# RWKV-7 state and gated MLP on one core: loads of chunks 4 and 5 moved between DMA queues, and the order of the weight words

## The chip, the cores and the metric

The kernel runs on one core of a Trainium2 chip. The metric is device time in microseconds. The engines of a core are TensorE (PE in the profile, with its weight loads as PEld), VectorE (DVE), ScalarE (ACT), GpSimd (POOL) and SyncE (SP). They run their own instruction streams side by side and wait for each other by semaphores. A DMA is issued by the queue of one of the engines; SyncE does nothing else here.

## The reference

Inputs are r, k, v, w, a, b of shape (4, 8, 768, 40): four batches, eight heads, 768 time steps, head size 40. For each head a 40 by 40 state is carried through time:

```python
y[:, :, t] = np.einsum('bhd,bhde->bhe', rt, state)
Sa = np.einsum('bhde,bhe->bhd', state, at)
state_decay = state * wt[:, :, None, :] - np.einsum('bhd,bhe->bhde', Sa, bt)
state = state_decay + np.einsum('bhd,bhe->bhde', vt, kt)
```

The y of all heads, laid side by side, is x of 3072 tokens by 320. An MLP follows, with weights of 320 by 2048 and 2048 by 320:

```python
h = x @ w_in
g = h * np.cos(h)
return (g @ w_out).astype(np.float32)
```

The two weight matrices come as 64-bit floats, all other inputs as 32-bit floats.

## The kernel before

**Chunks.** Time is cut into 24 chunks of 32 steps. Inside a chunk the recurrence is turned into matrix products and a triangular inverse; between chunks only the state (tile `qz`) is carried. A chunk's work is in small steps. `p1` prepares pairs of chunks from w, a and b: transposes, the running product of w, 1/w (`over_w`, L393), b/w (`bn`), a times the running product (`aT`), and their products (`nps`). `by_blocks` or `inverse` then inverts on VectorE for four chunks at a time; for chunks 0 to 3 the inverse is made in 16 by 16 blocks (`pair_step`), and `pair_first` and `pair_second` put the off-diagonal block together on TensorE, by way of two helper tiles `half` and `rn`. `p2` takes v, r and k (`p2_in` L564, `p2_kn` L572 on GpSimd, then transposes and `gram`). `main` is the chain through the state: `ch_t` (sT), `ch_q` (qps), `ch_x` (x0ps), `ch_s` (sps), `ch_z` (dps, then qz and yt). `tokens` (L749) writes yt to DRAM (xd) and reads it back transposed (xT), as the MLP's input.

**The weights.** Each weight is made into a 32-bit float from the two 32-bit words of its 64-bit float. There are 20 pieces of 512 columns by 128 rows, 512 KB of words each: for the first quarter of the MLP pieces 0 and 1 (w_in), 2 (the tail of w_in) and 3 to 5 (w_out), and so on; pieces 18 and 19 are the last 1024 columns of w_out as the kernel lays them out. A piece goes through four steps (`rounded`, L224): `fetch` (the words, L237, on SyncE's queue), `taken` (L245, L246 on VectorE, L249, L251 on ScalarE), `mantissa` (L255 VectorE, L258 ScalarE) and `product` (L261 VectorE, then the sign on GpSimd, L264). The words lie in buffers lent by other tiles: pieces 0 and 1 in gT, 2 in nt, 3 in u, 4 in inv, 5 and 6 in gT again, 7 in nt, 8 in u, 9 in inv, and from 10 on nt, u and inv in turn. So a fetch waits until the lender, or the piece before it, has let the buffer go.

**Memory that is used twice.** The weights' places are empty at first, and hold other things. The w and a of chunks 2 and 3 lie in w_in's second half, their b in the last 1024 columns of w_out (`late_out`). `half0` and `rn0`, the helper tiles of the inverse of chunks 0 to 3, lie in the 1536 columns before these (`spare`, L119 to L121): half0 under pieces 13 and 14, rn0 under piece 15. The upper part of half0 is set to zero at the start (L122). For w, a and b of all other chunks there are two tiles each, for even and odd chunks, so chunk 4's loads overwrite what chunk 0 left.

**Loads.** `load(c, names, via)` (L150) issues four DMAs of 40 KB for each name, one per batch (L156). From chunk 4 on w is not read from the input but from a DRAM tile `wd`, in which running products over time have been made ahead (`ws_fetch` L163, `ws_scan` L170, `ws_store` L182, for four chunks at a time). A load of w of chunk 4 or 5 has therefore to wait for the landing of that store.

**Order.** The order of all instructions is written out by hand. `step(work, of_inv, of_w)` (L346) issues one piece of work, then what has come due, then so many steps of the inverse and of the weights. `later(n, work)` (L343) makes work come due after n more steps. `landed` (L577) puts the next chunk's k, v and r in the list once the old ones have been read. A prologue handles chunks 0 to 3's preparation and most of chunk 0; then the loop over chunks goes through a list of segments, in which `M` is a place for a piece of the MLP. Work on one engine is done in this order, and SyncE issues its DMAs in it: one that waits for a buffer holds all behind it.

**Around the change.** In the prologue, `both_a` of chunk 2 (L870) puts six loads of four DMAs each in the list: w of chunks 4 and 5 and a of 4 after 8 steps, a of 5 and b of both after 9 (L879). They come due before chunk 2's k, v and r, which are put there by `p2_in(1)` after L970, and before pieces 3 and 4 of the weight words, fetched after the inverse. `shifted` (L944) issues small matmuls whose result is unused (tile pad), 121 of them in the prologue and 75 in chunk 19 (L973); `busy` issues others, of 512 columns. Most matmuls stand in two helpers, so the profile gives them the lines L101 (`mm`) and L330 (`turned`).

Of the kernel before, what the change touches and what calls it, by code (L numbers as in the profile page):

```python
# [20 lines left out]
def kernel(  # L21
# [43 lines left out]
    nc = tc.nc  # L65
    B, H, S, D = r.shape
    P, C, DP = 128, 32, 64
    HH = H // 2
    NCH = S // C
    DM, DFF = moe_w_in.shape  # L70
    NF = DFF // P
# [41 lines left out]
    w_out_sb = const.tile([P, NF, DM], F32, tag="w_out", name="w_out_sb")  # L113
# [2 lines left out]

    late = DFF - 2 * H * DP
    late_out = w_out_sb.rearrange("p f n -> p (f n)")[:, NF * DM - 2 * H * DP :]
    spare = w_out_sb.rearrange("p f n -> p (f n)")[:, NF * DM - 2 * H * DP - 3 * P * 4 : NF * DM - 2 * H * DP]  # L119
    half0 = spare[:, : 8 * P].rearrange("p (n t) -> p n t", t=C)  # L120
    rn0 = spare[:, 8 * P :].rearrange("p (n t) -> p n t", t=C // 2)  # L121
    nc.gpsimd.memset(half0[:, :, C // 2 :], 0.0)  # L122
    nat = {}
    for n, fill in (("w", 1.0), ("a", 0.0), ("b", 0.0)):
        for i in range(4):
            x = slice((i - 2) * H * DP, (i - 1) * H * DP)
            if i < 2:
                t = const.tile([P, H, DP], F32, tag=f"nat_{n}{i}", name=f"nat_{n}{i}")
            else:
                t = {  # L130
                    "w": w_in_sb[:, 0, late:], "a": w_in_sb[:, 1, late:], "b": late_out
                }[n][:, x].rearrange("p (h d) -> p h d", h=H)
# [4 lines left out]
    for n in "kvr":  # L137
        t = const.tile([P, H, D], F32, tag=f"nat_{n}", name=f"nat_{n}")
# [11 lines left out]
    def load(c, names, via=nc.sync):  # L150
        for n in names:
            for i in range(B):
                at_c = src[n][i, :, c * C : (c + 1) * C, :]
                if n == "w" and c >= 4:
                    at_c = wd[c // 4][i, :, c % 4]
                via.dma_start(nat[n, c][blk[i], :, :D], at_c.rearrange("h t d -> t h d"))  # L156
# [186 lines left out]
    def later(steps, work):  # L343
        waiting.append([steps, work])

    def step(work, of_inv=0, of_w=0, small=False):  # L346


        before = list(waiting)
        work()  # L350
        G["small"] = small
        for w in before:
            w[0] -= 1
            if w[0] == 0:
                waiting.remove(w)
                w[1]()
        for steps, n in ((inv_steps, of_inv), (w_steps, of_w)):
            for _ in range(min(n, len(steps))):
                steps.pop(0)()
# [67 lines left out]
    def p1_b(c):  # L427
        ps = at("bT")
        for i in range(2):
            turned(ps[:, i], bn_b[(c + i) % 7])  # L430
        for i in range(2):
            bT = sb3.tile([P, 4, P], F32, tag="opT", name="bT")
            nc.scalar.copy(bT.rearrange("p j t -> p (j t)"), ps[:, i])
            G["bT", c + i] = bT
# [427 lines left out]
    def p1(c):  # L862


        def first_w():
            p1_w(c)
            if c == 4:
                later(1, lambda: load(6, "w"))

        def both_a():  # L870
            p1_a(c)
            if c == 4:
                later(1, lambda: load(7, "w"))
                for i in range(2):
                    later(1, lambda i=i: load(6 + i, "ab"))
            elif c >= 2 and c + 3 < NCH:
                for m in range(6):
                    later(
                        8 + m // 3 if c == 2 else (9 if c == 6 else 2) + m, lambda m=m: load(c + 2 + m % 2, "wab"[m // 2])  # L879
                    )  # L880

        return [first_w, both_a, lambda: p1_b(c), lambda: p1_n(c)]

# [23 lines left out]
    with tc.manual_schedule():  # L907
# [36 lines left out]
        def shifted(n):  # L944


            ps = at("pad")
            for _ in range(n):
                mm(ps[:1, 0, :1], idle[:, :1], idle[:, :1], True)
# [4 lines left out]
        first, other = p1(0), p1(2)  # L954
        for seg in (*first[:2], *other[:2], *first[2:], *other[2:]):
            step(seg)
        for m in range(2):
            w_work[m][0]()
        scanned(1)
# [10 lines left out]
        w_work[2][0]()  # L970
        p2_in(1)
        p2_kn(1)
        N_PAD = {0: 121, 19: 75}  # L973
        shifted(N_PAD[0])
        while inv_steps:
            inv_steps.pop(0)()
# [35 lines left out]
        for c in range(NCH):  # L1012
            t, q, x, s, z = main(c)
            v, k, g = p2(c + 1) if c + 1 < NCH else [lambda: None] * 3
            q0 = c - c % 4 + 4
            fill, pn, pn4, parts, blocks = (1, 4), None, None, [], []
            if c == 0:
                segs = []
            elif c == 1:
                parts = [parts0[0], parts0[1]]  # L1020
                segs = [t, parts[0], v, q, parts[1], k, x, g, s, z]
                fill = (1, 4)
            elif c == 2:
                parts = parts0[2:]
                segs, fill = [t, parts[0], v, q, k, M, x, M, parts[1], g, M, s, M, z, M, M], (0, 3)
            elif c == 3:
                pw4, pa4, pb4, pn4 = p1(4)
                pw, pa, pb, pn = p1(6)
                segs = [
                    t, pw4, M, q, pa4, M, x, lambda: scanned(2), M, s, pw, M, pb4, pa, M, pn4, M, z, M,  # L1030
                    pb, v, pn, k, M, g,
                ]
                fill = (2, 3)
            elif c == 4:
                pw, pa, *p8 = p1(8)
                blocks = [
                    lambda n=n, f=f: f(4, *n) for n in ((0, 1), (1, 4)) for f in (pair_first, pair_second)
                ]
                segs = [
                    t, v, M, q, M, k, x, M, blocks[0], M, blocks[1], M, s, blocks[2], M, pw, blocks[3], M, z, M,  # L1040
                    g, M, pa, lambda: scanned(3),
                ]
                fill = (2, 0)
            elif c == 5:
                pw, pa = p1(10)[:2]
                pb, pn = p8
                segs = [t, M, pb, q, M, pn, k, M, x, M, s, pw, v, M, z, M, g, M, pa, M]
            elif c % 4 == 0 and q0 < NCH:
                pb, pn = p1(q0)[2:]
                segs = [t, v, M, q, M, k, x, M, g, M, s, pb, M, z, M, pn, M, M]  # L1050
                if q0 + 4 < NCH:
                    segs.insert(-1, lambda: scanned(c // 4 + 2))
            elif c % 4 == 1 and q0 < NCH:
                pw, pa = p1(q0 + 2)[:2]
                segs = [t, M, pw, q, M, x, k, M, s, v, M, z, M, pa, M, g, M, M]
            elif c % 4 == 2 and q0 < NCH:
                pb, pn = p1(q0 + 2)[2:]
                segs = [t, M, pb, q, M, pn, v, M, x, M, s, k, M, g, M, z, M, M]
            elif c % 4 == 3 and q0 + 4 < NCH:
                pw, pa = p1(q0 + 4)[:2]  # L1060
                segs = [t, M, pw, q, M, x, k, M, s, v, M, z, M, pa, M, g, M, M]
            else:
                segs = [t, v, M, q, M, x, k, M, g, M, s, M, M, z, M, M]
            n = len(segs)

            goal = 8 * (c + 1) - (18 if c < 19 else 20)
            empty, places = 0, segs.count(M)
            if c > 3:
                empty = max(0, min(places - (goal - done), 2 if c < 8 else places))
                goal = max(goal, done + places - empty)  # L1070
            place = 0
            if c == 19:
                shifted(N_PAD[c])
            for i, seg in enumerate(segs):
                while seg is s and ("rt", c) not in G:
                    if allowed(c):
                        piece(4, 0)
                    else:
                        inv_steps.pop(0)()
                while seg is pn4 and w_steps:  # L1080
                    w_steps.pop(0)()
                if seg is not M:
                    step(seg, *((0, 0) if seg in parts else fill), small=seg in (q, x, g, s, z, pn, pn4, *blocks))
                    if seg not in parts and (c < 2 or c == 2 and not done):
                        busy({s: 6, q: 5, v: 4, k: 4, z: 4}.get(seg, 3))
                else:
                    place += 1
                    if place * empty // places > (place - 1) * empty // places:
                        continue
                    if allowed(c) and (c != 4 or done < 23):  # L1090
                        piece(*fill)
                while i == n - 1 and c > 3 and done < goal and c != 4 and allowed(c):
                    piece(*fill)
                if seg is pn and (c == 3 or c > 4 and c % 4 == 2):
                    inv_steps.extend(by_blocks(q0) if c == 3 else inverse(q0))
# [36 lines left out]
```

## Time and profile before

| What | us |
|---|---|
| Median of three runs (823.66 to 827.18) | 825.35 |
| The profiled execution | 821.18 |
| Its span, first to last instruction | 819.5 |
| TensorE busy in the span | 756.6 (92%) |
| VectorE busy | 484.4 (59%) |
| ScalarE busy | 386.5 (47%) |
| GpSimd busy | 198.5 (24%) |

All times inside the kernel are those of the one profiled execution, counted from its first instruction. In the profile's lines the first figures are start and duration, then the engine, the line of the kernel, the operation, the tile written and the tile read, and how many instructions the entry merges; what stands in brackets is the time that the engine had been idle before, and what ended it. "SPq" is SyncE's queue of DMAs; the duration there is the time of issuing, not of the transfer. "issue" is time in which an engine waited for nothing that the profile shows. The mean granted clock of TensorE is 0.955 of its full speed. Moved in all: 55.79 MB, 51.95 of them by SyncE's queue (q1), 0.98 by ScalarE's (q10), 0.33 by GpSimd's (q0).

### The profile page before, as it was taken

To read this page: it belongs to the slowest core of one execution; us is meant where nothing else is said; L and a number is where in the kernel's file an instruction comes from. 1 tells how busy PE (TensorE), PEld (TensorE's weight loads), DVE (VectorE), ACT (ScalarE), POOL (GpSimd) and SP (SyncE) were. 2 spreads that over 40 slices of the span, in tenths; PEclk is the share of its full clock that TensorE was granted. 3 is DMA by queue.
4 is the path that set the end of the run, shared out by engine and by line. 5 is a ranking of instruction groups with operands and counts; after the bars stand their busy time and mean duration, and the time that the engine had idled before them with its cause. 6 is when DMAs were issued, how large, how long until landed. Compare 5 with 4: busy or idle time off the path is not lost.

```text
span 819.5 us, 39690 instructions
## 1 busy us (share of the span) xinstructions
PE 756.6 (92%) x17858; PEld 580.2 (71%) x17858; DVE 484.4 (59%) x1025; ACT 386.5 (47%) x720; POOL 198.5 (24%) x354
## 2 busy tenths in 40 slices
PE   3676787999899999999999999999999999999997
PEld 2653456677677777787777877777787777777775
DVE  6956667866364698454796554895445873332231
ACT  1324566654254544446345445435635435363352
POOL 5214352430214123221230330330230222201000
PEclk9856687999999999999999999999999999999999
DMA  7536554254144323334224314214220212101000
GB/s 122 126 83 177 160 143 115 45 126 73 29 103 92 67 52 61 70 90 75 54 38 71 73 59 72 53 38 68 59 40 25 45 39 51 21 19 36 19 17 16
DMA packets 183304, 55.79 MB, mean 68 GB/s; under 512 B 157152, under 2 KB 178656, under 8 KB 183136
## 3 DMA queue, kind: packets, MB, share of 16 engines
q1 hardware_dynamic: 180560, 51.95, 29.2%
q8 instruction: 140, 2.29, 1.2%
q10 hardware_dynamic: 2320, 0.98, 0.6%
q0 software_dynamic: 256, 0.33, 0.2%
q14 instruction: 28, 0.23, 0.1%
HBM read 42.07 MB, written 11.14 MB: 65 GB/s over the span
## 4 chain that ended last, share of the span: by engine, by line
PE 63%; DVE 14%; DMA 6%; ACT 5%; SPq 5%; issue 5%; POOL 2%; DVEq 0%; ACTq 0%; POOLq 0%
PE ph L101 22%; PE po L101 18%; SPq L156 4%; PE x0ps L101 3%; PE dps L101 3%; PE gram L101 3%; DVE inv_tmp L480 2%; PE vT L330 2%; DVE rw L395 2%; DVE inv L484 2%; PE nps L101 2%; PE sps L101 2%; PE qps L101 2%; DMA words<-in_moe_w_out_dram 1%; PE sT L634 1%
## 5 line engine op out<-in xcount | busy, mean ns | idle before, releaser
L101 PE MATMUL po<-w_out_sb,gT 128*128 128x320 f32 x768 | 223.2, 439 | 0.0
L101 PE MATMUL ph<-xT,w_in_sb 128*128 128x256 f32 x768 | 188.7, 391 | 2.8 <-issue 2.5
L101 PEld LDWEIGHTS po<-w_out_sb,gT 128*128 128x128 f32 x768 | 140.2, 190 | 54.2 <-issue 1.7
L101 PEld LDWEIGHTS ph<-xT,w_in_sb 128*128 128x128 f32 x768 | 141.2, 193 | 32.9 <-issue 14.9
L806 ACT ACTIVATE turns<-ph,rnd 128x512 f32<-128x512 f32 x96 | 64.1, 686 | 159.0 <-PE ph L101 158.6
L808 DVE SCALAR_TENSOR_TENSOR turns<-turns,ph 128x512 f32<-128x512 f32 x96 | 64.0, 684 | 117.4 <-ACT turns L806 117.1
L816 DVE TENSOR_TENSOR gT<-ph,turns 128x512 f32<-128x512 f32 x96 | 65.7, 686 | 37.5 <-ACT turns L813 37.5
L733 POOL TENSOR_TENSOR qz<-qz,wc 128x160 f32<-128x160 f32 x92 | 41.7, 472 | 158.3 <-DVE qz L732 157.7
L813 ACT ACTIVATE turns<-turns,half_pi 128x512 f32<-128x512 f32 x96 | 69.3, 722 | 3.1
L812 ACT ACTIVATE turns<-turns 128x512 f32<-128x512 f32 x96 | 60.2, 627 | 16.8 <-DVE turns L808 16.8
L101 PE MATMUL ph<-xT,w_in_tail 64*128 64x256 f32 x384 | 55.8, 410 | 0.0
L484 DVE TENSOR_TENSOR inv<-inv,inv_tmp 128x31 f32<-128x31 f32 (+15 forms) x124 | 50.8, 410 | 4.3
L566 POOL COPY vp<-nat_v 128x320 f32<-128x320 f32 x25 | 12.2, 486 | 160.5 <-DMA nat_v<-in_v_dram 134.4
L732 DVE TENSOR_TENSOR qz<-dps,qz 128x160 f32<-128x160 f32 x92 | 28.9, 314 | 35.6 <-PE dps L101 35.3
L480 DVE TENSOR_TENSOR inv_tmp<-u,inv 128x31 f32<-128x31 f32 (+15 forms) x124 | 48.2, 389 | 2.3
L395 DVE RECIPROCAL rw<-nat_w 128x320 f32<-128x320 f32 x20 | 42.8, 2141 | 0.0
L638 ACT COPY s<-sT 128x512 f32<-128x512 f32 x46 | 24.5, 584 | 37.1 <-PE sT L634 37.0
L101 PEld LDWEIGHTS ph<-xT,w_in_tail 64*128 64x128 f32 x384 | 33.8, 190 | 9.4 <-issue 5.5
L744 POOL TENSOR_TENSOR yt<-yt,wb 128x512 f32<-128x512 f32 x24 | 31.4, 1309 | 22.4 <-DVE yt L739 22.4
L634 PE MATMUL sT<-ident,qz 128*128 128x128 f32 x184 | 26.6, 287 | 5.6 <-POOL qz L733 2.9
L396 POOL TENSOR_TENSOR bn<-nat_b,rw 128x320 f32<-128x320 f32 x22 | 19.5, 887 | 48.8 <-DVE rw L395 41.6
L698 DVE TENSOR_TENSOR sm<-sps,su 128x128 f32<-128x128 f32 x48 | 11.7, 285 | 31.9 <-ACT sm L693 31.9
(136 smaller groups left out, 1108.4 us busy)
## 6 DMA issues: line engine op xcount, KB each, us to landing
words<-in_moe_w_in_dram SPq DMA_DIRECT2D x8, 512.0 KB
nat_k<-in_k_dram SPq DMA_DIRECT2D x96, 40.0 KB
nat_v<-in_v_dram SPq DMA_DIRECT2D x96, 40.0 KB
nat_r<-in_r_dram SPq DMA_DIRECT2D x96, 40.0 KB
xd<-yt SPq DMA_DIRECT2D x48, 80.0 KB
out_dram<-ot SPq DMA_DIRECT2D x24, 160.0 KB
nat_b<-in_b_dram SPq DMA_DIRECT2D x88, 40.0 KB
wd<-ws SPq DMA_DIRECT2D x5, 640.0 KB
```

The costliest lines, as they stand in the source:

```text
L101: nc.tensor.matmul(o, lhsT=lhsT, rhs=rhs, start=start, stop=stop, skip_group_check=True)
L156: via.dma_start(nat[n, c][blk[i], :, :D], at_c.rearrange("h t d -> t h d"))
L395: nc.vector.reciprocal(rw, wn)
L480: nc.vector.tensor_tensor(tmp, u[:, j : j + 1, :j].to_broadcast([P, C - j, j]), x[:, j:, j : j + 1].to_broadcast([P, C - j, j]), ALU.mult,)
L484: nc.vector.tensor_tensor(x[:, j:, :j], x[:, j:, :j], tmp, ALU.subtract)
L634: nc.tensor.transpose(ps[:, i // 4, (i % 4) * P : (i % 4 + 1) * P], qz[:, i // 2, i % 2, C : C + P], ident)
L733: nc.gpsimd.tensor_tensor(z, z, wc.rearrange("p (f m b) -> p f m b", f=2, m=2)[:, :, :, bb] .unsqueeze(3).to_broadcast([P, 2, 2, D]), ALU. ...
L806: nc.scalar.activation(n, u, ACTF.Identity, bias=rnd, scale=1.0)
L808: nc.vector.scalar_tensor_tensor(n, n, -ROUND, u, ALU.add, ALU.subtract)
L812: nc.scalar.activation(n, n, ACTF.Abs)
L813: nc.scalar.activation(n, n, ACTF.Sin, bias=half_pi, scale=-2.0 * math.pi)
L816: nc.vector.tensor_tensor(gT[:, 2 * e : 2 * e + 2].rearrange("p f t -> p (f t)"), us[e], ns[e], ALU.mult)
```

## The change

The a and b of chunks 4 and 5, 16 DMAs, are issued by GpSimd instead of SyncE, behind its copies for chunk 1 (`p2_kn(1)`). The w of chunks 4 and 5, 8 DMAs, stay with SyncE and are put in the list in chunk 1: four after five steps and four after seven. So the words of piece 2, chunk 2's k, v and r, and the words of pieces 3 and 4 no longer stand behind these 24 loads. `half0` moves to the last 1024 columns of w_out, under pieces 18 and 19 and over the b of chunks 2 and 3, and is therefore set to zero after these have been read; rn0 stays under piece 15. The pad of the prologue has 115 matmuls in place of 121.

```diff
-    spare = w_out_sb.rearrange("p f n -> p (f n)")[:, NF * DM - 2 * H * DP - 3 * P * 4 : NF * DM - 2 * H * DP]
-    half0 = spare[:, : 8 * P].rearrange("p (n t) -> p n t", t=C)
-    rn0 = spare[:, 8 * P :].rearrange("p (n t) -> p n t", t=C // 2)
-    nc.gpsimd.memset(half0[:, :, C // 2 :], 0.0)
+    half0 = late_out.rearrange("p (n t) -> p n t", t=C)
+    rn0 = w_out_sb.rearrange("p f n -> p (f n)")[:, NF * DM - 2 * H * DP - P * 4 : NF * DM - 2 * H * DP]
+    rn0 = rn0.rearrange("p (n t) -> p n t", t=C // 2)
...
-            elif c >= 2 and c + 3 < NCH:
+            elif c > 4 and c + 3 < NCH:
                 for m in range(6):
-                    later(
-                        8 + m // 3 if c == 2 else (9 if c == 6 else 2) + m, lambda m=m: load(c + 2 + m % 2, "wab"[m // 2])
-                    )
+                    later((9 if c == 6 else 2) + m, lambda m=m: load(c + 2 + m % 2, "wab"[m // 2]))
...
         for seg in (*first[:2], *other[:2], *first[2:], *other[2:]):
             step(seg)
+        nc.gpsimd.memset(half0[:, :, C // 2 :], 0.0)
         for m in range(2):
             w_work[m][0]()
...
         p2_kn(1)
-        N_PAD = {0: 121, 19: 75}
+        for c in (4, 5):
+            load(c, "ab", nc.gpsimd)
+        N_PAD = {0: 115, 19: 75}
         shifted(N_PAD[0])
...
             elif c == 1:
                 parts = [parts0[0], parts0[1]]
                 segs = [t, parts[0], v, q, parts[1], k, x, g, s, z]
+                later(5, lambda: load(4, "w"))
+                later(7, lambda: load(5, "w"))
                 fill = (1, 4)
```

## The prediction

> **What bounds the kernel now.** I read the stages first (busy time by stretch), to see where time can be won at all:
>
> ```profile
> 40.00:52.00 12.00, 9.59 (x248) 6.61 (x237) 9.09 (x26) 2.32 (x5) 2.77 (x5) 0.64 0.43 102
> 64.00:84.00 20.00, 12.42 (x283) 7.53 (x285) 13.53 (x18) 11.43 (x20) 9.81 (x10) 0.67 0.64 180
> 107.00:127.00 20.00, 14.13 (x307) 9.55 (x299) 13.66 (x22) 14.84 (x27) 9.68 (x8) 0.91 0.59 154
> 200.00:400.00 200.00, 194.20 (x5074) 151.89 (x5073) 117.19 (x247) 92.60 (x176) 44.39 (x84) 0.99 0.34 71
> ```
>
> After the length come busy PE, PEld, DVE, ACT, POOL, then the granted clock, DMA share and GB/s. From 200 us on TensorE is busy 97% of the time at clock 0.99: that part is bound by TensorE and written out in a fixed order, so whatever the first 150 us lose or win is carried to the end. Up to 127 us no engine is full. So I read there who waits (columns: us in total, times, longest):
>
> ```profile
> DVE mant L245 <- DMA words<-in_moe_w_out_dram: 13.0, 5, 6.2
> POOL vp L566 <- DMA nat_v<-in_v_dram: 11.0, 2, 6.8
> PE vT L330 <- POOL vp L566: 3.2, 1, 3.2
> DVE mant L245 <- DMA words<-in_moe_w_in_dram: 3.3, 2, 2.3
> ```
>
> VectorE waits 13.0 + 3.3 = 16.3 us for weight words (L245, the first step of a weight piece). The longest wait, 6.2 us, is at 67.8 to 74 us; GpSimd waits for chunk 2's v in the same place. The timeline of SyncE's DMA queue shows why both are late:
>
> ```profile
> 39.20 0.40 SPq L184 DMA_DIRECT2D wd<-ws  x1
> 44.29 4.31 SPq L156 DMA_DIRECT2D nat_w<-wd  x8
> 48.72 2.13 SPq L156 DMA_DIRECT2D nat_a<-in_a_dram  x4
> 50.96 3.51 SPq L237 DMA_DIRECT2D words<-in_moe_w_in_dram  x4
> 54.57 3.10 SPq L156 DMA_DIRECT2D nat_a<-in_a_dram  x4
> 57.72 4.86 SPq L156 DMA_DIRECT2D nat_b<-in_b_dram  x8
> 62.67 3.54 SPq L156 DMA_DIRECT2D nat_k<-in_k_dram  x4
> ...
> 68.23 1.94 SPq L156 DMA_DIRECT2D nat_r<-in_r_dram  x4
> 70.27 3.24 SPq L237 DMA_DIRECT2D words<-in_moe_w_out_dram  x7
> ...
> 74.89 0.92 SPq L753 DMA_DIRECT2D xd<-yt  x2
> 81.70 0.40 SPq L763 DMA_DIRECT2D xT<-xd  x1
> ```
>
> The queue stands from 39.6 to 44.29 for the store of wd, which chunk 4's w reads, then issues 24 loads that nothing uses before 149 us (chunk 3). Only then come chunk 2's k, v, r (62.67) and pieces 3 and 4 of the weight words (70.27). At 44 to 74 us the issue queue is the limit. The chain of waits agrees: it holds k and v issues from 63 us, the words of 70.70, and words again at 88.64, 96.38 and 120.22.
>
> **What the Trainium skill says.** "Perfetto Trace Analysis", DMA Optimizations: where the issuing engine looks full of DMA slices, spreading the DMAs over sync, scalar and GpSimd may help. The trace agrees that SyncE is such a queue: four loads take 1.9 us or more of it. "SBUF — State Buffer", Who interferes with whom: GpSimd writes descriptors through ports that a VectorE operation in a two-port mode locks, and tensor_tensor has no such mode. The trace shows GpSimd issues beside memsets, not beside VectorE's inversion. "Runtime: NRT & Kernel Launch", Instruction fetch mechanics: blocks of 256 instructions. The trace fits: TensorE stops 0.98 us inside the pad, and 382 matmuls (some 764 instructions, three blocks) later 1.85 us inside gram, with 7 of its 128 left.
>
> **The change part by part**, on the profiled execution (821.18 us, span 819.5).
>
> *SyncE.* The 16 a and b loads leave SyncE for good, the 8 w loads leave this place, and the wait for wd (4.6 us) goes with them. After the store at 39.6: piece 2's four words, 3.5 us, to 43.1; k as soon as GpSimd has read the old k (kn ends at 43.4 us; 43.9 with the moved memset), then v and r, 1.93 us each for four, to about 50; piece 3 (its buffer u is free by 48.5), piece 4 after the transpose that ends at 51.7, done by 53.3. Landing took 3.1 us (70.70 to 73.8): ready at 56 to 57. VectorE wants piece 3 at 67.8. The whole 6.18 us wait goes, with 11 us to spare; GpSimd's wait for v and r and TensorE's for vp go with it. What is late next is ScalarE: piece 2's product needs its mantissa, now about 69.5 us, against a product at 75.45 before. Gain here **5.9 us**.
>
> *Next on SyncE.* Piece 6's words wait for a buffer that VectorE leaves at 64.8. Then yt, ready at 66.0, is stored there and not at 74.89; its way back (xT, held 5.8 us by that store) is issued by 72.7, and piece 7 at about 74.5 instead of 83.39: 8.9 us earlier. But chunk 1 now holds the 8 w loads, four ahead of v and four ahead of piece 10: 8 by 0.49 = 4.0 us (1.93 for four, k or v row), up to 4.9 at the slow rate of the nat_b row. Piece 7 lands about 79.5 (5.3 us as before), VectorE wants it at 81.5: that wait of 1.0 us goes. Piece 9, issued by 89.3, lands 92 against 99.1: 7 us or a little more. Piece 10, issued 90.6 against 96.38, landed 8.7 us after issue in a crowd of three 512 KB pieces; the crowd now begins earlier and moves at the same 150 to 160 GB/s, so about 98 against 105.1. From there each piece's words wait for the buffer that the one before leaves, so the queue and VectorE shift together: **7.0 us** from the chunk's end on, 5.9 of it the first wait and 1.1 the later ones.
>
> *GpSimd.* 16 issues. The only row is at the start: 7 in 4.02 us, 0.58 each; 16 by 0.58 = 9.3 us. They start where vvm ends (43.84, 44.3 with the memset) and end at 53.6:
>
> ```profile
> 3.99 4.02 POOL L156 DMA_DIRECT2D w_in_sb<-in_a_dram  x7
> 43.34 0.50 POOL L574 COPY vvm<-nat_v 128x320 f32<-128x320 f32 x1
> 60.20 1.16 POOL L264 TENSOR_TENSOR w_in_sb<-w_in_sb,sign 128x512 f32<-128x512 f32 x1 [16.36 <-DVE w_in_sb L261]
> ```
>
> GpSimd sat idle until 60.2, so this costs nothing with 6.6 us to spare. Behind the issues stand piece 0's sign product (60.2), then the state's product qz (62.55), which is on the chain: past 60 us every us of delay costs one. The data is used at about 150 us. Contention with VectorE: inversion steps are tensor_tensor; two-port forms are the four tensor_scalar of 0.40 to 0.42 us at 51.5 to 53.8. Bound: nothing, up to 2 us if steps slow as they did beside GpSimd's copies at 41 to 43.6 us (0.82 for 0.27). I take 0.
>
> *The memset of half0* (0.53 us) moves from the start to behind inv at 29.7; vp, kn and so k's issue move 0.5 us. TensorE is in nps until 32.8 and takes vT after it; vp still ends at 30.7. Cost 0; without that cover 0.5.
>
> *half0 and rn0.* TensorE's second pair product of chunk 2 waited 2.8 us for GpSimd's product of piece 14, whose words overlay half0. That wait goes, since half0 now lies under pieces 18 and 19. ScalarE is filled without a break from 125.0 to 132 us by piece 15 and the cosines, so I take 0; the bounds are 0 and 2.8 us.
>
> *Pad.* VectorE's 1.82 us gap before 47.23 is a tick memset waiting for TensorE's read, which stands behind the pad. Six fewer at 1.41/51 = 28 ns: 0.17 us. It also moves each instruction block six matmuls: the 1.85 us stop falls with 1 matmul of gram left. By that count it stays: 0; if one instruction more drops out, it passes gram and up to 1.85 us are won.
>
> Sum: 5.9 + 1.1 + 0.2 = **7.2 us**, 821.18 to 814.0. The median of the runs before, 825.35, lies 4.2 us above the profiled execution; I take the same difference off it: **818.2 us**.
>
> **The rivals.**
> - *The queue keeps the gain small.* The 8 w loads in chunk 1 take 4.9 us there and the words of pieces 8 to 12 are bound by transfer (160 to 180 GB/s at 64 to 107 us), so that only a third to a half of the gain reaches 107 us: 2.5 to 3.5 us, about 822.4. For it: piece 10's 8.7 us landing. Against: the transfers begin 7 us earlier too.
> - *More is won:* the 1.85 us stop passes gram and half of the 2.8 us wait counts: 7.2 + 1.9 + 1.4 = 10.5 us, 814.9.
> - *Slower: GpSimd becomes the bound.* If an issue takes longer beside VectorE's work than the 0.58 us at the start, the stream runs into piece 0's product and qz. It touches them from (60.2 - 44.3)/16 = 0.99 us an issue, eats the whole gain at 1.44, and is 0.5% slower at 1.70. At 1.9 us: 14.5 - 7.2 = 7.3 us more, 832.6. "SBUF — State Buffer" (section "A bandwidth-pool intuition that's wrong (but worth ruling out)") has some 620 ns for such a DMA alone and 3100 ns beside a VectorE copy, so it is possible; against it, the window holds only four short operations of the locking kind.
> - *The loads aren't needed sooner, nothing moves.* Excluded for words and k, v, r by the waits above.
>
> **How the numbers follow.** A kernel whose three runs span 0.43% can tell about 0.5%, 4.1 us, from no change. Chances: the forecast (5 to 9.5 us won) 0.54; more 0.16; small (0 to 5 us) 0.20, of which 0.04 above 4.1; slower, GpSimd or stops of TensorE's fetch put in worse places, 0.10, of which 0.07 beyond 0.5%. So faster 0.74, same 0.19, slower 0.07. Range: 813.5 (11.9 won) to 823.5 (1.9 won), which leaves out the slower case and the lowest of the small one, and a little above 10.5; the forecast alone spans 815.9 to 820.4.
>
> **What would show it.** Piece 3's and 4's words issued near 50 us; no wait before mant at 67.8; 16 issues on GpSimd from 44 to 54 and idle time left before its product at about 60; xd near 66; w of chunks 4 and 5 between 80 and 91; chunk 3's sT near 140 in place of 147.3. It is wrong if GpSimd's product of piece 0 comes after 61, if mant waits anew for words after 88 us, or if TensorE's idle time after 150 us (653.4 us busy of 669 now) grows.

## The result and the profile after

The change made no difference that can be measured: 821.39 us median (816.67 to 825.88, 20 runs) against 821.12 (816.92 to 827.18, 20 runs) before, a ratio of 0.9991 with a 95% interval of 0.9973 to 1.0008. My likeliest case was 7.2 us less. The profiled execution's span is 822.0 us.

Busy time by stretch of the changed kernel (length, then busy PE, PEld, DVE, ACT, POOL, then TensorE's clock, DMA share, GB/s):

```profile
40.00:52.00 12.00, 8.90 (x193) 6.24 (x194) 7.33 (x27) 1.84 (x4) 10.35 (x19) 0.57 0.77 176
52.00:64.00 12.00, 5.34 (x329) 3.98 (x327) 5.73 (x11) 4.62 (x10) 1.56 (x3) 0.75 0.75 210
64.00:84.00 20.00, 15.23 (x502) 10.28 (x505) 17.39 (x28) 11.66 (x21) 13.09 (x14) 0.81 0.41 112
```

The kernel before, at 52 to 64 us:

```profile
52.00:64.00 12.00, 7.61 (x395) 6.39 (x384) 5.60 (x19) 3.90 (x8) 2.61 (x5) 0.50 0.45 89
```

From 40 to 52 us the transfers went from 102 to 176 GB/s, and TensorE and VectorE did less in the same time; at 52 to 64 us VectorE was busy 5.7 us, much as before, and TensorE 5.34 in place of 7.61. From 64 us VectorE is fuller, 17.4 us in place of 13.5; but a second profile of the kernel before has 17.1 there, so this figure alone shows no gain. SyncE's queue issued its loads in the order that was forecast, but piece 4's words, which wait for a transpose, only by 57.5 us, where 53.3 had been reckoned:

```profile
40.31 2.80 SPq L236 DMA_DIRECT2D words<-in_moe_w_in_dram  x4
43.98 2.35 SPq L155 DMA_DIRECT2D nat_k<-in_k_dram  x4
...
49.22 2.14 SPq L155 DMA_DIRECT2D nat_r<-in_r_dram  x4
51.53 6.96 SPq L236 DMA_DIRECT2D words<-in_moe_w_out_dram  x7
58.53 0.60 SPq L164 DMA_DIRECT2D ws<-in_w_dram  x1
...
71.19 0.70 SPq L752 DMA_DIRECT2D xd<-yt  x2
...
81.87 2.66 SPq L155 DMA_DIRECT2D nat_w<-wd  x4
```

and GpSimd's 16 issues took 9.2 us, from 44.36, with 11.85 us idle behind them:

```profile
44.36 2.32 POOL L155 DMA_DIRECT2D nat_a<-in_a_dram  x4
...
51.26 2.30 POOL L155 DMA_DIRECT2D nat_b<-in_b_dram  x4
65.42 1.16 POOL L263 TENSOR_TENSOR w_in_sb<-w_in_sb,sign 128x512 f32<-128x512 f32 x1 [11.85 <-DVE w_in_sb L260]
```

In the waits of the changed kernel (total, times, longest) only one for weight words is left, in chunk 2:

```profile
DVE mant L244 <- DMA words<-in_moe_w_out_dram: 5.2, 1, 5.2
```

So the 16.3 us of waits fell to 5.2 (11.2 and 3.9 in a second profile of each kernel), and still the time stood. But the product at 65.42 stood at 60.20 before: all is 5 us late by then. TensorE's own timeline, where "issue" is a stop for which no engine is to blame, shows why:

```profile
46.37 1.26 PE L101 MATMUL pad<-idle 128*1 128x1 bf16 x45 [2.08 <-issue]
...
58.59 0.27 PE L101 MATMUL sps<-x,rt 32*32 32x72 f32 x1 [1.83 <-issue]
...
63.14 0.21 PE L101 MATMUL gram<-rT,vT 40*32 40x32 f32 x1 [2.75 <-issue]
```

From sps to gram one matmul and 127 more lie between the stops; with the weight load of each that makes 256 instructions, one block. Before, the stops were 0.98 in pad, none in sps and 1.85 in gram:

```profile
43.17 1.41 PE L101 MATMUL pad<-idle 128*1 128x1 bf16 x51 [0.98 <-issue]
...
57.79 0.33 PE L101 MATMUL gram<-rT,vT 40*32 40x32 f32 x7 [1.85 <-issue]
```

**Where the time went.** The first sT of each chunk cuts the execution into parts. Two profiles of each kernel, in us:

| Part | before | before, again | after | after, again | change of the means |
|---|---|---|---|---|---|
| start to sT of chunk 1 | 63.2 | 64.7 | 68.4 | 69.0 | +4.8 |
| chunk 1 | 39.4 | 36.7 | 30.7 | 31.0 | -7.2 |
| chunk 2 | 44.7 | 43.9 | 45.0 | 43.7 | +0.1 |
| chunk 3 | 38.3 | 39.2 | 41.7 | 41.1 | +2.6 |
| chunk 4 | 40.5 | 38.6 | 41.1 | 40.3 | +1.1 |
| chunks 5 to 12 | 238.1 | 240.4 | 238.9 | 239.6 | 0.0 |
| chunk 13 | 28.5 | 28.5 | 29.6 | 30.0 | +1.3 |
| the rest of the span | 326.7 | 328.6 | 326.6 | 326.4 | -1.1 |

The sum, +1.5, is the difference of the mean spans (820.1 to 821.6). The forecast gain is there, in chunk 1; 4.8 us were lost ahead of it and 3.7 in chunks 3 and 4. Of the 4.8, 0.9 us are there already at the first x0ps, ahead of the pad (at 39.4 us on the mean before, at 40.3 after); the other 3.9 us were lost behind it, where these stops lie.

### The profile page after: what moved, and what is told of

Read it like the earlier page. It is cut to its first block, busy times and chain, and to the rows that moved or that the text cites. A ratio compares the mean times of both kernels' runs of the same rounds, so it can differ in the third digit from the quotient of the medians.

```text
span 822.0 us, 39694 instructions
## 1 busy us (share of the span) xinstructions
PE 752.6 (92%) x17852; PEld 578.0 (70%) x17852; DVE 486.3 (59%) x1025; ACT 386.7 (47%) x720; POOL 209.2 (25%) x370
## 4 chain that ended last, share of the span: by engine, by line
PE 63%; DVE 15%; ACT 6%; issue 6%; DMA 4%; SPq 3%; POOL 1%; DVEq 0%; ACTq 0%; POOLq 0%
PE ph L101 22%; PE po L101 18%; PE dps L101 3%; PE x0ps L101 3%; SPq L155 3%; PE gram L101 2%; DVE inv_tmp L479 2%; PE vT L329 2%; DVE rw L394 2%; DVE inv L483 2%; PE nps L101 2%; PE sps L101 2%; PE qps L101 2%; PE bT L329 1%; PE sT L633 1%
## 5 line engine op out<-in xcount | busy, mean ns | idle before, releaser
L101 PEld LDWEIGHTS ph<-xT,w_in_sb 128*128 128x128 f32 x768 | 142.4, 194 | 35.9 <-issue 16.4
L731 DVE TENSOR_TENSOR qz<-dps,qz 128x160 f32<-128x160 f32 x92 | 28.8, 313 | 36.7 <-PE dps L101 32.8
L637 ACT COPY s<-sT 128x512 f32<-128x512 f32 x46 | 24.5, 584 | 36.9 <-PE sT L633 36.8
L649 ACT COPY qz<-qps 40x512 f32<-40x512 f32 x46 | 26.6, 579 | 8.9 <-PE qps L101 8.4
```

Of the source, the lines that this page charges most:

```text
L101: nc.tensor.matmul(o, lhsT=lhsT, rhs=rhs, start=start, stop=stop, skip_group_check=True)
L731: nc.vector.tensor_tensor(z, pick(dp, 0, (2 * N72 + C, 2), (N72, 2), (1, D)), z, ALU.add)
```

## The experiments

The theory: TensorE's instruction blocks are fetched by the same DMA system, and the transfers that the change brings forward slow them ("fetch theory"). Rivals: the stops just differ from one execution to the next; or their place, set by the pad, is what counts.

**Both kernels profiled again**, unchanged.

> The kernel before, profiled a second time. Measures how far one profile of a kernel differs from another. Fetch theory (TensorE's stops inside a run of matmuls grow with the DMA traffic beside them, and the change raises that traffic at 40 to 64 us): stops between 25 and 66 us near the 4.0 us of the first profile, first sT (chunk 1) within 1 us of 63.2. Chance theory (the stops just differ from one execution to the next): the sum anywhere from 4 to 9 us, first sT up to 5 us off.

> The changed kernel, profiled a second time. Fetch theory: stops between 25 and 66 us again 7 to 9 us, first sT again 66 to 69 us, and chunk 2's sT again near 99. Chance theory: stops fall back to about 4 us in this one, first sT near 63 to 64.

Stops between 25 and 66 us: 5.1 us (before: 3.9 the first time); 10.5 us (after: 8.8). The first sT of the two pairs lies 5 us apart, and 1.5 us at most within a pair. Chance is not the whole explanation for these pairs, but single stops move by up to 2 us; a wider scatter comes at the end of this section.

**Traffic alone, small loads.** The kernel before, with a copy of GpSimd's 16 loads added:

```diff
         p2_kn(1)
+        for c in (4, 5):
+            for m, n in enumerate("ab"):
+                o = (2 * (c - 4) + m) * H * D
+                dst = w_out_sb.rearrange("p f n -> p (f n)")[:, o : o + H * D].rearrange("p (h d) -> p h d", h=H)
+                for i in range(B):
+                    nc.gpsimd.dma_start(dst[blk[i]], src[n][i, :, c * C : (c + 1) * C, :].rearrange("h t d -> t h d"))
```

> The kernel before, with the 16 loads of a and b of chunks 4 and 5 issued a second time by GpSimd at the place of the change, into a part of w_out that nothing has filled yet. Nothing else is moved: only traffic and GpSimd's issues are added. Fetch theory: TensorE's stops at 40 to 64 us grow from 2.8 us by 2 to 4 us, first sT at 65 to 67.5; time 0 to 4 us more. Chance theory, or alignment by the pad: stops at 40 to 64 us stay within 1 us of 2.8, first sT near 63, time the same.

Stops in pad, sps and gram: 4.6 us (1.5 + 0.7 + 2.4), against 2.8 and 3.1. First sT 65.3. Ratio to before 1.0009 (0.9989 to 1.0029). A stop in sps appeared; the growth of 1.5 to 1.8 us is at the lower end or below, so these loads are at most the smaller part.

**Traffic alone, weight words at 44 us.** The kernel before, with 1 MB more:

```diff
         p2_kn(1)
+        for i in range(2):
+            nc.gpsimd.dma_start(
+                w_out_sb.rearrange("p f n -> p (f n)")[:, i * 2 * WID : (i + 1) * 2 * WID].bitcast(I32),
+                moe_w_in[i * P : (i + 1) * P, 3 * WID : 4 * WID].bitcast(I32),
+            )
```

> The kernel before, with 1 MB of weight words (two DMAs of 512 KB with long rows) read by GpSimd at the place of the change into a part of w_out that nothing has filled yet; only traffic is added. Fetch theory, now with large transfers as the heavier cause: stops at 40 to 64 us (pad, sps, gram) grow from 2.8 to 3.1 us to 4.5 to 7, a stop in sps appears, first sT at 65.5 to 68. Rival (the change's order of instructions or the place of the stops lengthens them, traffic does not): stops near 3 us, first sT near 64.

A miss: pad 0.71, gram 1.85, none in sps. First sT 65.2, but with a stop of 2.1 us in nps that lies ahead of the added loads. The megabyte raised the traffic at 40 to 52 us to 180 GB/s and was gone after it (79 GB/s at 52 to 64). The single time was 828.56 us; in its profile chunk 3 took 44.5 us and began at a low clock (wT at 1.77 us), so that time is not the added loads' alone. If traffic matters, it is the traffic while a block is on its way, and the block of sps and gram is wanted after 55 us.

**Traffic alone, weight words at 54 us.** So the same with 2 MB, issued by ScalarE behind its copy of half:

```diff
                 step(lambda: pair_first(0, 0, 1))
+        nc.scalar.dma_start(
+            w_out_sb.rearrange("p f n -> p (f n)")[:, : 4 * WID].bitcast(I32), moe_w_in[:P, : 2 * WID].bitcast(I32)
+        )
+        nc.scalar.dma_start(
+            w_in_sb[:, :, 2 * WID :].bitcast(I32),
+            moe_w_in[: 2 * P, :WID].bitcast(I32).rearrange("(i p) n -> p i n", p=P),
+        )
```

> The kernel before, with 2 MB of weight words read in two DMAs that ScalarE issues behind its copy of half at 51 us, into parts of w_in and w_out that hold nothing then. The traffic at 52 to 64 us rises from 80 or 90 GB/s to about 200, as in the changed kernel; nothing else changes there but two issues on ScalarE. Fetch theory (a block's fetch is slowed by the transfers that run while it is on its way): stops in sps and gram grow from 1.9 to 2.4 us to 4 to 7, a stop in sps appears, first sT 66 to 69. Rival (traffic does nothing, the change's own order does): sps and gram 2 to 3 us, first sT 63.5 to 65.5.

TensorE's waits at 40 to 70 us, of the kernel before and of this one:

```profile
PE gram L101 <- issue: 1.9, 1, 1.9
...
PE pad L101 <- issue: 1.0, 1, 1.0
```

```profile
PE gram L101 <- issue: 6.0, 1, 6.0
...
PE pad L101 <- issue: 0.7, 1, 0.7
```

The stop in pad, ahead of the added transfers, stayed; the one in gram, beside them (253 GB/s at 58 to 64 us; in the kernel before 106 at 52 to 58 us, where its stop lies), went from 1.9 to 6.0 us. First sT 70.4, of which some 1.3 us come from a long stop in nps at 34 us. Time 832.07 in one run, against a median of 823.01 of the kernel before beside it. The stop in sps that was expected with it did not appear. Instructions and block ends of TensorE are those of the kernel before, so the rival of the place falls here.

The trace also holds the transfers of the instructions themselves: packets of 16 KB of the kind "instruction", on queue q8. The DMA queues of this kernel (packets, MB, share of 16 engines), at 56.8 to 62 us and then at 62 to 63.4 us:

```profile
q10 hardware_dynamic: 353, 1.60, 82.1%
q1 hardware_dynamic: 320, 0.19, 16.4%
...
q8 instruction: 1, 0.02, 5.6%
```

The instructions for which gram stops began to move at 62.1 us, when ScalarE's words (q10) were all but through, 5.3 us after the first matmul of the block ahead of them; in the kernel before it was 1.1 us. The packet itself took 1.3 us here and 1.2 there. So it is the wait of the packet that grew, and not its transfer. This holds wider: in the fourteen profiles of this document each of the 37 stops in pad, sps and gram ends 1.2 to 1.8 us after such a packet has landed, and from the first matmul of the block ahead (128 matmuls back) to the end of the stop it is never under 3.7 us. The matmuls from sps to gram run for 1.7 to 1.9 us, so gram stops even without added traffic. In the two profiles of the changed kernel these packets waited 1.9 to 4.3 us, in the two of the kernel before 1.1 to 1.9.

**The change without GpSimd's loads.** a and b issued by SyncE at the end of chunk 2:

```diff
-        for c in (4, 5):
-            load(c, "ab", nc.gpsimd)
...
                 segs, fill = [t, parts[0], v, q, k, M, x, M, parts[1], g, M, s, M, z, M, M], (0, 3)
+                for m in range(4):
+                    later(12 + m, lambda m=m: load(4 + m % 2, "ab"[m // 2]))
```

> The changed kernel, with a and b of chunks 4 and 5 issued by SyncE at the end of chunk 2, where its queue stands idle, instead of by GpSimd at 44 us. 640 KB of traffic leave the stretch at 44 to 56 us. Fetch theory: the stops at 40 to 64 us fall from 6.7 us to 3 to 5, first sT 64 to 66.5, the kernel 2 to 4 us faster than the changed one, 3 to 5 us faster than before if the later gain stays. Chance or alignment: stops and first sT as in the changed kernel, time within 1 us of it.

Stops in pad, sps and gram 6.1 us (after: 6.7 and 8.6), first sT 67.4, ratio to before 0.9975 (0.9954 to 0.9995). Most of the stops stayed, with the words still early; stops and first sT are outside what the fetch theory had said. As a time it is not clear of the changed kernel.

**121 pads on the changed kernel.**

```diff
-        N_PAD = {0: 115, 19: 75}
+        N_PAD = {0: 121, 19: 75}
```

> The changed kernel with 121 pad matmuls in place of 115, so that TensorE's instruction blocks end where they ended before. Fetch theory: stops at 40 to 64 us stay at 6 to 9 us, first sT 68 to 69.5; chunk 13 takes 28.5 us again in place of 29.6 to 30.0, so about 1.2 us are won later; time 0 to 2 us less than the changed kernel. Alignment theory: the stops at 40 to 64 us fall to about 3 us too, first sT near 64, time 4 to 6 us less than the changed kernel.

First sT 68.3; stops in pad, sps and gram 5.3 us, somewhat under the 6 to 9 expected; ratio 0.9995 (0.9977 to 1.0013). The place of the blocks does not by itself cause the early loss. Chunk 13 is 28.5 us again, but it was 28.5 and 28.8 too in two kernels below with 115 pads, so the pad does not settle that one.

**All 24 loads late.** w of chunks 4 and 5 too at the end of chunk 2:

```diff
-                later(5, lambda: load(4, "w"))
-                later(7, lambda: load(5, "w"))
...
-                for m in range(4):
-                    later(12 + m, lambda m=m: load(4 + m % 2, "ab"[m // 2]))
+                for m in range(6):
+                    later(12 + m // 2, lambda m=m: load(4 + m % 2, "wab"[m // 2]))
```

> The changed kernel with all 24 loads of chunks 4 and 5 (w, a and b) issued by SyncE at the end of chunk 2. Fetch theory: first sT as with a and b late (67 to 68), chunk 1 unchanged or up to 1 us shorter because 8 issues leave its queue; time as with a and b late or up to 2 us less, unless w lands too late for chunk 3, which its first wT would show. Rival (the 8 w loads in chunk 1 cost the gain): 3 us or more less than with a and b late.

Chunk 1 took 30.6 us, with w in it 30.5: the 8 w loads in chunk 1 cost nothing. First sT was 69.9, not the expected 67 to 68, with stops of 7.0 us in pad, sps and gram; up to there the instructions are those of the kernel with a and b late (67.4 and 6.1), so this difference is scatter. Ratio 0.9984 (0.9961 to 1.0006).

**a and b late, 121 pads.** The two edits together.

> a and b at the end of chunk 2 on SyncE, and 121 pad matmuls. Fetch theory with the two small parts added: first sT 67 to 68, chunk 1 about 30.5 us, chunk 3 about 40.5, chunk 13 28.5: 1.2 us less than a and b late alone, so some 3 to 4 us less than before. Alignment theory: first sT near 64, 6 us or more less than before.

First sT 66.8, chunk 1 30.5, chunk 3 40.6, chunk 13 28.5. Ratio 0.9962 (0.9942 to 0.9982), 819.54 us: the gain is within what was expected and clear of no change, but not of the changed kernel (0.9973 to 1.0008).

**The fetch of w for later chunks taken away from 58 us.** On the changed kernel:

```diff
-            later(12, lambda: ws_fetch(q + 1))
+            later(34 if q == 1 else 12, lambda: ws_fetch(q + 1))
```

> The changed kernel, with the 640 KB fetch of w for the products over time of chunks 8 to 11, which nothing needs before 159 us, issued at the end of chunk 2 in place of 58.5 us. Fetch theory: with 640 KB less at 58 to 64 us the stop in gram falls from 2.6 to 4.7 us to about 2, first sT at 66.5 to 68, chunk 1 as before; the kernel 0.5 to 2.5 us faster than the changed one. Rival: gram's stop stays at 2.6 to 4.7 us, time the same.

Gram stopped 2.3 us, at the low end, but sps 3.3, so together 5.6: no shorter than in the changed kernel (4.6 and 7.1). Busy time of this kernel by stretch:

```profile
52.00:58.00 6.00, 2.28 (x150) 1.72 (x138) 1.96 (x5) 3.41 (x7) 1.73 (x3) 0.52 1.00 258
58.00:64.00 6.00, 2.74 (x179) 2.17 (x162) 1.93 (x5) 0.61 (x3) 0.28 (x1) 0.50 0.15 51
```

The words, with the last of GpSimd's loads, held the transfers at 258 GB/s and full share while sps's block was wanted; behind them, at 51 GB/s, the later stop was short. First sT 67.0, where no stop in nps occurred this time; ratio 0.9976 (0.9958 to 0.9995).

**All three edits** (a and b late, the fetch late, 121 pads).

> a and b and that fetch at the end of chunk 2 on SyncE, and 121 pad matmuls. Fetch theory: traffic at 52 to 64 us falls to about 150 GB/s, sps and gram stop 2 to 3 us together, first sT 65 to 66.5, chunk 1 near 30.5 us, chunk 3 near 40.5; ratio to the kernel before 0.993 to 0.996. Rival: as with a and b late and 121 pads, 0.996.

Stops: pad 0.7, gram 2.1, none in sps; first sT 64.8, ratio 0.9960 (0.9942 to 0.9977), 820.48 us. It is as good as the one without the late fetch, not better.

**The clock in chunk 3.** The same kernel, with 12 matmuls that add zeros while TensorE waits for the state:

```diff
+            if c == 3:
+                for _ in range(12):
+                    mm(G["po", 0], idle, pick(idle, 0, (0, 4), (1, DM // 4)), False, False)
```

> As the kernel with a and b and the late fetch at the end of chunk 2 and 121 pads, with 12 matmuls more before chunk 3 that add zeros to the MLP's open sum, in the 2 us in which TensorE waits for the state. Clock theory (chunk 3 takes 2 us more in the changed kernels because TensorE's clock drops after that wait): the clock stays at 1.00 at the start of chunk 3, its first wT takes 1.04 us in place of 1.5 to 1.9 and ph 1.9 in place of up to 3.2, chunk 3 takes 38.5 to 40 us in place of 41.4; ratio to the kernel before 0.993 to 0.996. Rival (chunk 3 is set by the landing of the a loads on SyncE's queue, the clock costs nothing): wT and ph faster, but chunk 3 again 40.5 to 41.5 us, ratio 0.996.

TensorE in chunk 3, of the changed kernel and then of this one:

```profile
146.17 1.49 PE L329 MATMUL wT<-ident,nat_w 128*128 128x128 f32 x8
147.45 3.19 PE L101 MATMUL ph<-xT,w_in_sb 128*128 128x256 f32 x8
```

```profile
145.71 1.06 PE L329 MATMUL wT<-ident,nat_w 128*128 128x128 f32 x8
146.61 1.89 PE L101 MATMUL ph<-xT,w_in_sb 128*128 128x256 f32 x8
...
165.76 1.08 PE L329 MATMUL aps<-ident,nat_a 128*128 128x128 f32 x4 [2.81 <-DMA nat_a<-in_a_dram]
166.64 3.13 PE L101 MATMUL ph<-xT,w_in_sb 128*128 128x256 f32 x8
```

The slow start of chunk 3 did not occur here, but the chunk took 41.6 us all the same: TensorE now waits 2.81 us for the a of chunk 7, and ph behind that wait takes the 3.13 us. The clock over the whole chunk was 0.96, as in the changed kernel, so the low clock only came later, and the run doesn't decide between the two theories. The ratio is 1.0031 (1.0010 to 1.0053), slower than without, where neither theory had expected it.

The profile doesn't explain that, but it shows how far one profile can be trusted. Up to chunk 3 this kernel runs the instructions of the one above, yet its stops in pad, sps and gram are 6.9 us and not 2.8, and its first sT is at 68.5 and not 64.8 (from chunk 3's sT to the last one it takes 604.4 us against 603.9). That is nearly as much as the whole early loss. So the short stops of "all three edits" may be luck, and the experiments that took loads away don't show which of them cost how much. What stands against chance is the whole set: eight of the nine profiles with the early words have their first sT at 66.8 us or later, and of the five without, only the one with the 2 MB.

## Why the prediction was right and wrong

**SyncE's queue and the words: right in the main.** The order came as worked out, and the times from 65 us on 1 to 5 us later (xd at 71.2 for 66.0, piece 9 by 90.4 for 89.3). Chunk 1 fell by 7.2 us on the mean, for 5.9 + 1.1 expected, and the long wait is gone. That the sum fits so well is in part luck: against the single profiles of the kernel before the fall is 8.5 and 5.9 us. In part it may have another cause, too: TensorE's mean clock in chunk 1 was 0.67 and 0.64 before, 0.78 and 0.72 after, and its same 700 matmuls took 27.2 us on the mean before and 23.6 after. No run separates this. The w loads in chunk 1 cost nothing that shows (30.6 without, 30.5 with them), where I had charged 4.0 us of queue.

**GpSimd: right.** 0.58 us an issue, done at 53.6. The inversion steps beside them took 0.24 to 0.28 us, as without, which agrees with the page "SBUF — State Buffer" (Who interferes with whom), where it is given for tensor_tensor as inferred. The rival of a slow stream did not occur.

**The memset, half0's wait: right.** No step waits for the memset, and the second pair product of chunk 2 no longer waits for piece 14. Chunk 2 took as long as before (+0.1), so nothing was won there, as taken. What this wait alone was worth isn't shown, since other things in chunk 2 changed with it: VectorE waited 5.2 and 3.9 us for words (5.8 and 3.4 before), and TensorE was busy some 4 us less.

**The step that failed: the pad and the block stops.** I asked only where the stop falls. That was exact (one matmul of gram left), but I priced it by its length before ("By that count it stays: 0"), and took the other ends as hidden. The stops became longer: in pad, sps and gram 6.7 and 8.6 us against 2.8 and 3.1. "Runtime: NRT & Kernel Launch" (Instruction fetch mechanics) says that crossing a block is mostly hidden; here it is not, beside 200 GB/s or without (1.85 us beside 106). They grew by 4.7 us on the mean, which covers the 3.9 us lost between the first x0ps and the first sT. That traffic lengthens a stop is shown by the added words (1.9 to 6.0 us, with the packet waiting behind them); that the change's own transfers made all of the 3.9 us isn't: taking 640 KB away at either place shortened the stops by no more than they scatter.

**"What the first 150 us win is carried to the end": wrong too.** After chunk 2 the lead over the kernel before was still 2.3 us; chunks 3 and 4 took 3.7 us more. TensorE starts chunk 3 at a low clock in seven of the nine profiles of kernels with the early words (wT at 1.49 to 1.92 us). But the kernel with only the fetch of w late started it at 1.06 and took 40.9 us, and the one with the zeros 41.6: a good start did not bring the time back. Over the whole chunk the clock was 1.00 in both profiles before and 0.96 in both after, and TensorE was busy 36.0 and 35.9 us before, 37.8 and 37.5 after; in chunk 4, at 0.96 and then 0.92, 36.9 and 36.5 before, 37.9 and 37.0 after. So some 2.4 of the 3.7 us are TensorE's work taking longer, and the rest is waiting. What lowers the clock, and whether the time would come back with it, stays open, as does chunk 13's 1.3 us.

**The signs.** Of those that I had named as showing me wrong, two came: GpSimd's product of piece 0 at 65.4 us, after 61, and mant's new wait for words at 117.9, after 88. The third doesn't decide: TensorE's idle time after 150 us was 16.0 and 19.6 us before, 18.2 and 19.0 after. Chunk 3's sT was at 144.1, not near 140.

**The rivals, and luck.** The measured time is inside the range, at the place of "the queue keeps the gain small", but no gain was measured, and that the time lies there is luck. The range was laid off from 825.35 us, the median of three runs; the kernel before had 821.12 in twenty. From there the same range (1.9 to 11.9 us won) would have ended at 819.2, below the 821.39 measured. Nor was the mechanism that rival's: the gain was made in chunk 1 and paid for elsewhere. Only "slower" (0.10) thought of the stops, by their places and not by their length, and "same" got 0.19.

## What to carry to other kernels

Before a transfer is moved forward, look at what runs beside its new place: stops that the profile calls "issue" on TensorE can grow with the traffic (here from 1.85 to 5.97 us), and in a stretch where the other engines wait for TensorE they lie on the path. The packets of kind "instruction" tell whether such a stop is a wait for instructions. A wait that is removed is worth its length only up to the next thing that the same edit makes later. With stops that scatter by up to 2 us each, and by 4 us in sum, profile both kernels twice or more and compare part by part, before one line is believed.

## What was not expected of the hardware

- One and the same instruction stop of TensorE, in gram with 7 of its 128 matmuls left, took 1.85 us with 106 GB/s beside it (at 52 to 58 us) and 5.97 us with 253 GB/s (at 58 to 64 us).
- 1 MB of added words at 44 us left the stops after 55 us as they were (gram 1.85 us), 2 MB at 54 us trebled gram's (5.97). In these runs the moment counted, not only the sum. But the traffic's rate does not fix a stop: with the same instructions and 143 and 135 GB/s at 52 to 64 us, two kernels stopped for 2.8 and 6.9 us.
- What grew in the long stop was the time before the 16 KB packet of instructions started (5.3 us for 1.1); the packet took 1.3 us for 1.2.
- A wait of 2.0 to 2.1 us on TensorE ahead of chunk 3 was followed by transposes of 1.49 to 1.92 us in place of 1.04 in seven profiles of kernels with the early words, but not in that of the kernel with only the fetch of w late, where after the same wait they took 1.06. With 1 MB of words added to the kernel before, a wait of 1.7 us was enough (1.77). So the length of the wait alone does not decide.
